# Softmax denominators of a hash-attention kernel: one sum per pair of heads on four quarters of TensorE's columns, spread by transfers

## The chip, the cores and the metric

The kernel runs on one core of a Trainium2 chip. The metric is device time in microseconds (us); the time before is the median of three runs, 891.09 us (890.82 to 892.35). TensorE multiplies matrices (PE in the profile, with PEld for its weight loads), VectorE (DVE), ScalarE (ACT) and GpSimd (POOL) work on elements, and SyncE (SP) issues most transfers. [...]

## What is computed

Hash attention for 4 batches x 8 heads, 768 queries and keys of 64 elements, followed by a feed-forward block with a quick GELU (cut to what matters):

```python
mask = q_bucket[:, :, :, None] == k_bucket[:, :, None, :]      # buckets: 6 sign bits of q @ proj, k @ proj
scores = scale * np.matmul(q, k.transpose(0, 1, 3, 2))
scores = np.where(mask, scores, -1000000000.0)
scores = scores - np.max(scores, axis=-1, keepdims=True)
attn = np.exp(scores)
attn = attn / (np.sum(attn, axis=-1, keepdims=True) + 1e-09)
attn_out = np.matmul(attn, v)
# x: (4 * 768, 512) from attn_out
h = x @ w_in                                   # 512 -> 2048
g = h * (1.0 / (1.0 + np.exp(-1.702 * h)))
out = g @ w_out                                # 2048 -> 512
```

The division by the sum of exponentials is the part that the change touches.

## The kernel before

Two heads make a pair (heads 2hp and 2hp+1 of one batch), so there are 16 pairs, n = 0 to 15. Keys lie on the 128 partitions and queries along the row; the 768 queries of a pair are taken in two halves of 384, c = 0 and c = 1. D is 64, P is 128, T is 6 tiles of 128 keys, GT is 3, HS is 384. One turn of the main loop (a "group") is one half of one pair; for the first pair it is a half of a half.

In group (n, c) TensorE first makes six tiles of scores, each from a product of hash features (bf16, kf and qf) and a product of keys and queries (f32), and ScalarE takes the exponential of each. The sums over keys are made in two parts: GpSimd adds the first three tiles of exponentials, VectorE the last three and GpSimd's result, one group later. What is left, a sum over the 128 partitions, is a product with a matrix of ones on TensorE (`total`), one for each head of the pair.

```python
            def scores(n, c, kts):
                qT, kT, qf, kf = xts[n, "q"], xts[n, "k"], feats[n % 2]["q"], feats[n % 2]["k"]
                cols = slice(c * HS, (c + 1) * HS)
                for kt in kts:
                    ps = sps.tile([P, 2, 512], F32, tag="s", name="ps")
                    keys = slice(kt * P, (kt + 1) * P)
                    for a, m, last in ((kf, qf, False), (kT, qT, True)):
                        for j in range(2):
                            hs = slice(D * j, D * (j + 1))
                            nc.tensor.matmul(ps[:, j, 0:HS], a[hs, keys], m[hs, cols], start=not last, stop=last)
                    nc.scalar.activation(es[c][:, kt, :, 0:HS], ps[:, :, 0:HS], Act.Exp, scale=1.0 / D**0.5)
```
```python
            def add_high(n, c):
                e = [es[c][:, GT + i, :, 0:HS] for i in range(GT)]
                acc = accs[n, c] = st.tile([P, 2, HS], F32, tag="acc", name="acc", bufs=1)
                nc.vector.scalar_tensor_tensor(acc, e[0], T * TINY, e[1], op0=Alu.add, op1=Alu.add)
                for x in (e[2], accs.pop((n, c, 0))):
                    nc.vector.tensor_tensor(acc, acc, x, op=Alu.add)
                # ... (values(): the product of exponentials and v, 12 matmuls into av)
            def x_of(n, c):
                b, hp = pairs[n]
                x = xT[:, hp, b * S : (b + 1) * S]
                x = x.rearrange("d (t p) -> d t p", p=P) if n else x.rearrange("d (p t) -> d t p", p=P)
                return x[:, c * GT : (c + 1) * GT, :]

            def unload(n, c):
                av = avs.pop((n, c))
                vs = st.tile([P, 1], F32, tag="vs", name="vs")
                nc.scalar.copy(vs, av[:, HS : HS + 1])
                nc.scalar.activation(x_of(n, c), av[:, 0:HS].rearrange("p (t s) -> p t s", t=GT), Act.Identity, bias=vs[:, 0:1])

            def total(n, c):
                acc = accs.pop((n, c))
                dn = accs[n, c] = mps.tile([P, HS], F32, tag="m", name="dn")
                for j in range(2):
                    nc.tensor.matmul(dn[D * j : D * (j + 1), :], ones, acc[:, j, :], start=True, stop=True)

            def invert(n, c):


                dn = accs.pop((n, c))
                rt = st.tile([P, HS], F32, tag="rt", name="rt")
                nc.vector.transpose(rt, dn)
                r = st.tile([P, HS // 32, 1], F32, tag="r", name="r")
                nc.vector.reciprocal(r, rt.rearrange("p (s i) -> p s i", i=32)[:, :, 0:1])
                accs[n, c] = rt, r

            def spread(n, c):
                rt, r = accs[n, c]
                nc.vector.transpose(rt.rearrange("p (s i) -> p s i", i=32), r.to_broadcast([P, HS // 32, 32]))

            def norm(n, c):
                rt, r = accs.pop((n, c))
                nc.vector.tensor_tensor(x_of(n, c), x_of(n, c), rt.rearrange("p (t s) -> p t s", t=GT), op=Alu.mult)
```

`total` fills a PSUM tile `dn` whose 64 rows per head are all the same sum, `invert` turns it in blocks of 32x32 so that each sum lies in one element of a row and takes the reciprocal of 12 elements, `spread` turns it back into rows, and `norm` multiplies the output of the attention.

The hash features of the next pair are made in the same groups: `hashed` is a product for four quarters of TensorE's columns (two halves of k, two of q), `featured` makes the features with one VectorE instruction and sends them to their partitions with eight small transfers of 12 partitions each. The first four (kf and qf of half 0 among them) must have landed before the first scores of the next pair.

```python
            def hashed(n):

                h = dots[n] = mps.tile([P, HS], F32, tag="m", name="hash")
                for i, x in enumerate("kq"):
                    for c in range(2):
                        r0 = D * i + 32 * c
                        nc.tensor.matmul(h[r0 : r0 + 32, :], pf[x], xts[n, x][:, c * HS : (c + 1) * HS],
                                         start=True, stop=True)

            def featured(n):
                f = wk.tile([P, HS], BF16, tag="f", name="f", bufs=1)
                nc.vector.tensor_scalar(f, dots.pop(n), above[:, 0:1], weight[:, 0:1], op0=Alu.is_gt, op1=Alu.mult)
                for c in range(2):
                    for i, x in enumerate("kq"):

                        queue = nc.scalar if (n, x) == (1, "q") else nc.sync
                        for j in range(2):
                            r0 = D * i + 32 * c + 2 * NB * j
                            queue.dma_start(out=feats[n % 2][x][D * j : D * j + 2 * NB, c * HS : (c + 1) * HS],
                                            in_=f[r0 : r0 + 2 * NB, :])
```

The weights w_in come as 64-bit floats and are converted in the same groups, one chunk of 128x512 per pair (`convert`, a generator that `step` moves on; each `yield` ends a step):

```python
        raw = cv.tile([P, CW, 2], U32, tag="raw", name="raw")
        (queue or loader[0]).dma_start(out=raw, in_=src)

        def of(x):
            return x if len(dst.shape) == 2 else x.rearrange("p (x r) -> p x r", r=dst.shape[2])

        lo, hi = raw[:, :, 0], raw[:, :, 1]
        bits = cv.tile([P, CW], U32, tag="bits", name="bits")
        part = (cv if psum is None else psum).tile([P, CW], U32, tag="part", name="part")
        size = (cv if psum is None else psum).tile([P, CW], F32, tag="size", name="size")
        yield
        # 1: part = (hi << 3) & mask            VectorE
        # 2: bits = (hi & 0xC0000000) | part    VectorE
        # 3: part = bits & 0xFF800000           VectorE;   size = hi * hi   ScalarE
        # 4: part = lo * 2**-52 * part          VectorE
        # 5: dst = bits + part                  VectorE
        # 6: dst = (size >= ...) * dst          VectorE
```

The loop:

```python

                if hashes:
                    featured(hashes.pop())
                ended = prev and prev[2][-1] == T - 1
                if ended:
                    add_high(*prev[:2])
                    totals.append((g + (g == len(groups) or len(kts) == GT), prev[:2]))
                for x in norms:
                    spread(*x)

                turned = ("", "k", "q", "")[g] if n == 0 else "kq" if c == 0 and n < last else ""
                for x in turned:
                    turn(n + 1, x)
                    measure(n + 1, x)
                if c == 1 or n == 0:
                    while norms:
                        norm(*norms.pop(0))
                inverted = []
                while totals and totals[0][0] == g:
                    inverted.append(totals.pop(0)[1])
                    total(*inverted[-1])
                    invert(*inverted[-1])
                while norms:
                    norm(*norms.pop(0))
                norms += inverted
                if prev:
                    values(*prev)
                if ended:
                    unload(*prev[:2])
                if "q" in turned:
                    hashed(n + 1)
                    if n:
                        hashes.append(n + 1)
                    else:
                        featured(n + 1)
                    for x in "kq":
                        if n + 2 <= last:
                            fetch(n + 2, x)
                    fetch_v(n + 1)
                if kts and kts[-1] == T - 1:
                    step(n, 4 - c)
                    if c == 0 and n > last - len(x_sums):
                        x_sums[n - last - 1]()
                    if c == 1:
                        begin(n + 1)
                if g == len(groups) - 1:
                    guard(0)
                if g == len(groups):
                    guard(1)
```

The transfers of the loop are issued by SyncE, in an order that the program's build has fixed: before the change, for each pair, four of k and four of q (of the pair after the next), two of v, eight of features, one of w_in.

Of the kernel before, what the change touches and what calls it, by code (L numbers as in the profile page):

```python
# [8 lines left out]
F32 = mybir.dt.float32  # L9
# [10 lines left out]
P = 128  # L20
# [18 lines left out]
def kernel(  # L39
# [118 lines left out]
    def convert(cv, dst, src, queue=None, psum=None):  # L158
# [10 lines left out]
        part = (cv if psum is None else psum).tile([P, CW], U32, tag="part", name="part")  # L169
        size = (cv if psum is None else psum).tile([P, CW], F32, tag="size", name="size")  # L170
# [109 lines left out]
    def attention(ff):  # L280
# [4 lines left out]
        with actx:  # L285
# [154 lines left out]
            def add_high(n, c):  # L440
                e = [es[c][:, GT + i, :, 0:HS] for i in range(GT)]
                acc = accs[n, c] = st.tile([P, 2, HS], F32, tag="acc", name="acc", bufs=1)
                nc.vector.scalar_tensor_tensor(acc, e[0], T * TINY, e[1], op0=Alu.add, op1=Alu.add)
                for x in (e[2], accs.pop((n, c, 0))):
                    nc.vector.tensor_tensor(acc, acc, x, op=Alu.add)  # L445
# [10 lines left out]
            def x_of(n, c):  # L456
                b, hp = pairs[n]
                x = xT[:, hp, b * S : (b + 1) * S]
                x = x.rearrange("d (t p) -> d t p", p=P) if n else x.rearrange("d (p t) -> d t p", p=P)
                return x[:, c * GT : (c + 1) * GT, :]  # L460

            def unload(n, c):
                av = avs.pop((n, c))
                vs = st.tile([P, 1], F32, tag="vs", name="vs")
                nc.scalar.copy(vs, av[:, HS : HS + 1])  # L465
                nc.scalar.activation(x_of(n, c), av[:, 0:HS].rearrange("p (t s) -> p t s", t=GT), Act.Identity, bias=vs[:, 0:1])  # L466

            def total(n, c):
                acc = accs.pop((n, c))
                dn = accs[n, c] = mps.tile([P, HS], F32, tag="m", name="dn")  # L470
                for j in range(2):
                    nc.tensor.matmul(dn[D * j : D * (j + 1), :], ones, acc[:, j, :], start=True, stop=True)  # L472

            def invert(n, c):


                dn = accs.pop((n, c))
                rt = st.tile([P, HS], F32, tag="rt", name="rt")
# [3 lines left out]
                accs[n, c] = rt, r  # L482

            def spread(n, c):
                rt, r = accs[n, c]
                nc.vector.transpose(rt.rearrange("p (s i) -> p s i", i=32), r.to_broadcast([P, HS // 32, 32]))

            def norm(n, c):
                rt, r = accs.pop((n, c))
                nc.vector.tensor_tensor(x_of(n, c), x_of(n, c), rt.rearrange("p (t s) -> p t s", t=GT), op=Alu.mult)  # L490
# [34 lines left out]
            for g in range(len(groups) + 2):  # L525
# [13 lines left out]
                if ended:  # L539
                    add_high(*prev[:2])  # L540
                    totals.append((g + (g == len(groups) or len(kts) == GT), prev[:2]))
                for x in norms:
                    spread(*x)
# [5 lines left out]
                if c == 1 or n == 0:  # L549
                    while norms:  # L550
                        norm(*norms.pop(0))
                inverted = []
                while totals and totals[0][0] == g:
                    inverted.append(totals.pop(0)[1])
                    total(*inverted[-1])
                    invert(*inverted[-1])
                while norms:
                    norm(*norms.pop(0))
                norms += inverted
# [14 lines left out]
                if kts and kts[-1] == T - 1:  # L574
                    step(n, 4 - c)
# [12 lines left out]
            for x in norms:  # L588
                spread(*x)
                norm(*x)  # L590
# [408 lines left out]
```

## Time and profile before

| | |
|---|---|
| time | 891.09 us |
| span of the profiled run | 888.7 us |
| TensorE busy | 873.2 us (98%) |
| VectorE busy | 709.3 us (80%) |
| ScalarE busy | 313.9 us (35%) |
| GpSimd busy | 309.7 us (35%) |
| TensorE in the attention (60 to 340 us) | 279.13 of 280 us |
| sum products `dn` (L472) on the last chain | 3% of the span |

The attention takes the first 335 us, the feed-forward block the rest. A row of the groups names the line of the kernel, the engine, the output and inputs, and the mean time of one instruction. An f32 matmul appears as two records, and matmuls on different columns of TensorE lie over each other, so the time of a step is read from the starts of what follows, not from the sum of durations. A transfer's row (SPq) is the time in which SyncE issues it; the data land later.

### The profile page before, as it was taken

Reading aid. Unit: us, or ns where it says so; the run is one execution under the profiler, and the core shown is the slowest. Engines: PE = TensorE matmul, PEld = TensorE weight load, DVE = VectorE, ACT = ScalarE, POOL = GpSimd, SP = SyncE. Lnnn points to the kernel's source line nnn. Section 1 sums busy time; section 2 is a strip of 40 time slices with the busy share of each in tenths; the row PEclk is TensorE's granted clock in tenths of the full one; section 3 lists DMA queues with packets and bytes.
Section 4 is the critical chain, followed back from the end, with each engine's and each line's share of the span. In section 5 each row is a group of like instructions: output and inputs, shape, how many; then the busy total and the mean of one; then the engine's idle time right before and its main releaser. Section 6 shows DMA issues by size and latency. Waiting matters only on the chain.

```text
span 888.7 us, 11969 instructions
## 1 busy us (share of the span) xinstructions
PE 873.2 (98%) x4077; PEld 503.5 (57%) x4077; DVE 709.3 (80%) x1020; ACT 313.9 (35%) x519; POOL 309.7 (35%) x275
## 2 busy tenths in 40 slices
PE   9899999999999999999999999999999999999995
PEld 4444444444444444444444444444888888888884
DVE  4698887888889964777788787888798977897785
ACT  5755666666665642233222223322100000000000
POOL 4243233222333263666434435559932000000000
PEclk9999999999999999999999999999999999999998
DMA  4745544556544103555455545565845665467524
GB/s 103 122 83 84 103 81 81 86 98 96 97 83 82 46 1 107 188 191 189 177 209 194 201 155 202 189 236 194 301 156 190 190 210 216 159 220 237 190 96 97
DMA packets 169477, 132.01 MB, mean 149 GB/s; under 512 B 123936, under 2 KB 138432, under 8 KB 164032
## 3 DMA queue, kind: packets, MB, share of 16 engines
q1 hardware_dynamic: 167712, 129.69, 51.0%
q10 hardware_dynamic: 1696, 1.48, 0.6%
q8 instruction: 34, 0.56, 0.3%
q14 instruction: 35, 0.29, 0.1%
HBM read 79.69 MB, written 50.33 MB: 146 GB/s over the span
## 4 chain that ended last, share of the span: by engine, by line
PE 96%; DVE 2%; DMA 1%; ACTq 0%; issue 0%; SPq 0%; ACT 0%; DVEq 0%
PE product L699 32%; PE product L812 28%; PE ps L429 16%; PE av L453 14%; PE dn L472 3%; PE hash L405 1%; DMA q<-in_q_dram 1%; PE tp L363 0%; ACTq L417 0%; DVE xT L816 0%; PE warm L356 0%; PE hash L370 0%; DVE y L791 0%; DVE acc L445 0%; SPq L325 0%
## 5 line engine op out<-in xcount | busy, mean ns | idle before, releaser
L430 ACT ACTIVATE e<-ps 128x768 f32<-128x768 f32 x192 | 151.5, 813 | 19.3 <-PE ps L429 13.4
L429 PE MATMUL ps<-qT,kT 64*128 64x384 f32 x768 | 155.1, 482 | 0.0
L699 PE MATMUL product<-xT,w_in_sb 128*128 128x512 f32 x288 | 135.4, 592 | 0.0
L453 PE MATMUL av<-e,v 128*64 128x385 f32 x768 | 130.2, 486 | 0.9 <-ACT xT L466 0.9
L437 POOL TENSOR_TENSOR acc<-e 128x768 f32<-128x768 f32 x32 | 49.6, 1551 | 208.1 <-ACT e L430 103.3
L707 ACT ACTIVATE c<-c 128x512 f32<-128x512 f32 x72 | 45.5, 632 | 186.2 <-issue 78.8
L453 PEld LDWEIGHTS av<-e,v 128*64 128x64 f32 x768 | 54.9, 136 | 70.5 <-issue 69.0
L699 PEld LDWEIGHTS product<-xT,w_in_sb 128*128 128x128 f32 x288 | 54.6, 190 | 68.5 <-issue 63.4
L699 PE MATMUL product<-t_x,s_in 128*128 128x512 f32 x192 | 90.2, 592 | 0.0
L429 PEld LDWEIGHTS ps<-qT,kT 64*128 64x128 f32 x768 | 68.2, 188 | 35.5 <-issue 35.5
L216 POOL TENSOR_TENSOR v<-c,u 128x512 f32<-128x512 f32 x24 | 34.3, 1427 | 129.2 <-ACT c L707 129.2
L818 ACT COPY u<-product 128x256 f32<-128x256 f32 x21 | 7.8, 373 | 167.7 <-PE product L812 125.6
L429 PE MATMUL ps<-qf,kf 64*128 64x384 bf16 x384 | 63.0, 324 | 0.7 <-ACT e L430 0.5
L699 PEld LDWEIGHTS product<-t_x,s_in 128*128 128x128 f32 x192 | 36.5, 190 | 45.9 <-issue 43.8
L438 POOL TENSOR_TENSOR acc<-acc,e 128x768 f32<-128x768 f32 x32 | 56.7, 1772 | 2.5
L699 PE MATMUL product<-xT,s_in 128*128 128x512 f32 x96 | 45.1, 592 | 0.0
L699 PE MATMUL product<-t_x,w_in_sb 128*128 128x512 f32 x96 | 45.1, 592 | 0.0
L429 PEld LDWEIGHTS <-kf 64*128 64x128 bf16 x384 | 18.9, 94 | 42.2 <-issue 20.7
L479 DVE STREAM_TRANSPOSE rt<-dn 128x384 f32<-128x384 f32 x32 | 18.6, 580 | 25.7 <-PE dn L472 25.6
L465 ACT COPY vs<-av 128x1 f32<-128x1 f32 x32 | 5.1, 160 | 95.0 <-PE av L453 94.9
L812 PE MATMUL product<-raw_g,xT 128*128 128x256 f32 x152 | 35.1, 379 | 0.0
L490 DVE TENSOR_TENSOR xT<-xT,rt 128x384 f32<-128x384 f32 x32 | 32.6, 1020 | 1.7
(201 smaller groups left out, 1558.3 us busy)
## 6 DMA issues: line engine op xcount, KB each, us to landing
raw_g<-g_dram SPq DMA_DIRECT2D x22, 1024.0 KB
s_in<-g_dram SPq DMA_DIRECT2D x20, 1024.0 KB
g_dram<-c SPq DMA_DIRECT2D x72, 256.0 KB
g_dram<-t SPq DMA_DIRECT2D x48, 256.0 KB
raw<-in_moe_w_out_dram SPq DMA_DIRECT2D x16, 512.0 KB
raw<-in_moe_w_in_dram SPq DMA_DIRECT2D x15, 512.0 KB
v<-in_v_dram SPq DMA_DIRECT2D x32, 192.0 KB
g_dram<-u SPq DMA_DIRECT2D x24, 256.0 KB
```

The costliest lines, as they stand in the source:

```text
L216: return [lambda: eng.tensor_tensor(t1, b12, b11, op=Alu.subtract), lambda: eng.tensor_tensor(b12, b22, b12, op=Alu.subtract), lambda: eng ...
L429: nc.tensor.matmul(ps[:, j, 0:HS], a[hs, keys], m[hs, cols], start=not last, stop=last)
L430: nc.scalar.activation(es[c][:, kt, :, 0:HS], ps[:, :, 0:HS], Act.Exp, scale=1.0 / D**0.5)
L437: nc.gpsimd.tensor_tensor(acc, es[c][:, 0, :, 0:HS], es[c][:, 1, :, 0:HS], op=Alu.add)
L438: nc.gpsimd.tensor_tensor(acc, acc, es[c][:, 2, :, 0:HS], op=Alu.add)
L453: nc.tensor.matmul(av[D * j : D * (j + 1), :], vt[:, t, j, :], es[c][:, t, j, :], start=(t == 0), stop=(t == T - 1))
L472: nc.tensor.matmul(dn[D * j : D * (j + 1), :], ones, acc[:, j, :], start=True, stop=True)
L479: nc.vector.transpose(rt, dn)
L490: nc.vector.tensor_tensor(x_of(n, c), x_of(n, c), rt.rearrange("p (t s) -> p t s", t=GT), op=Alu.mult)
L699: nc.tensor.matmul(ps, wq[LEFT[i]][:, kc, :], xq[RIGHT[i]][:, kc, :], start=(kc == 0), stop=(kc == K2 - 1))
L707: nc.scalar.activation(c, c, Act.Gelu_apprx_sigmoid)
L812: nc.tensor.matmul(ps, wq[LEFT[i]][:, c, :], gq[RIGHT[i]][:, c, :], start=(c == 0), stop=(c == F4 - 1))
```

## The change

Both halves of a pair's queries are summed in one step, at the first group of the next pair. The product of ones uses 32 columns instead of 64, so that head j and half c get the 32 rows from 64j + 32c on, four products on four quarters of TensorE's columns. One pass of `invert` then does both halves and turns the reciprocals back at once; each quarter holds 32 equal rows. Eight transfers of 32 partitions x 384 (48 KB each) copy them to the 64 rows of each head and half in `rs`, and one `norm` per pair multiplies 128x768. It saves sums on TensorE and instructions on VectorE. To make room in SBUF, `convert` keeps `part` in its destination and the square in place of the high word, and its steps are split 2 and 4 over the two groups of a pair, where they were 4 and 3. `acc` gets two buffers, since two are now alive at a time.

```diff
@@ -166,8 +166,11 @@
 
         lo, hi = raw[:, :, 0], raw[:, :, 1]
         bits = cv.tile([P, CW], U32, tag="bits", name="bits")
-        part = (cv if psum is None else psum).tile([P, CW], U32, tag="part", name="part")
-        size = (cv if psum is None else psum).tile([P, CW], F32, tag="size", name="size")
+        if psum is None:
+            part, size = dst.bitcast(U32), hi.bitcast(F32)
+        else:
+            part = psum.tile([P, CW], U32, tag="part", name="part")
+            size = psum.tile([P, CW], F32, tag="size", name="size")
         yield
 
 
@@ -439,7 +442,7 @@
 
             def add_high(n, c):
                 e = [es[c][:, GT + i, :, 0:HS] for i in range(GT)]
-                acc = accs[n, c] = st.tile([P, 2, HS], F32, tag="acc", name="acc", bufs=1)
+                acc = accs[n, c] = st.tile([P, 2, HS], F32, tag="acc", name="acc")
                 nc.vector.scalar_tensor_tensor(acc, e[0], T * TINY, e[1], op0=Alu.add, op1=Alu.add)
                 for x in (e[2], accs.pop((n, c, 0))):
                     nc.vector.tensor_tensor(acc, acc, x, op=Alu.add)
@@ -453,41 +456,44 @@
                         nc.tensor.matmul(av[D * j : D * (j + 1), :], vt[:, t, j, :], es[c][:, t, j, :],
                                          start=(t == 0), stop=(t == T - 1))
 
-            def x_of(n, c):
+            def x_of(n):
                 b, hp = pairs[n]
                 x = xT[:, hp, b * S : (b + 1) * S]
-                x = x.rearrange("d (t p) -> d t p", p=P) if n else x.rearrange("d (p t) -> d t p", p=P)
-                return x[:, c * GT : (c + 1) * GT, :]
+                return x.rearrange("d (t p) -> d t p", p=P) if n else x.rearrange("d (p t) -> d t p", p=P)
 
             def unload(n, c):
                 av = avs.pop((n, c))
                 vs = st.tile([P, 1], F32, tag="vs", name="vs")
                 nc.scalar.copy(vs, av[:, HS : HS + 1])
-                nc.scalar.activation(x_of(n, c), av[:, 0:HS].rearrange("p (t s) -> p t s", t=GT), Act.Identity, bias=vs[:, 0:1])
-
-            def total(n, c):
-                acc = accs.pop((n, c))
-                dn = accs[n, c] = mps.tile([P, HS], F32, tag="m", name="dn")
-                for j in range(2):
-                    nc.tensor.matmul(dn[D * j : D * (j + 1), :], ones, acc[:, j, :], start=True, stop=True)
-
-            def invert(n, c):
-
-
-                dn = accs.pop((n, c))
-                rt = st.tile([P, HS], F32, tag="rt", name="rt")
+                nc.scalar.activation(x_of(n)[:, c * GT : (c + 1) * GT, :], av[:, 0:HS].rearrange("p (t s) -> p t s", t=GT), Act.Identity, bias=vs[:, 0:1])
+
+            def total(n):
+
+                dn = accs[n] = mps.tile([P, HS], F32, tag="m", name="dn")
+                for c in range(2):
+                    acc = accs.pop((n, c))
+                    for j in range(2):
+                        r0 = D * j + 32 * c
+                        nc.tensor.matmul(dn[r0 : r0 + 32, :], ones[:, 0:32], acc[:, j, :], start=True, stop=True)
+
+            def invert(n):
+
+
+                dn = accs.pop(n)
+                rt = st.tile([P, HS], F32, tag="rt", name="rt", bufs=1)
                 nc.vector.transpose(rt, dn)
                 r = st.tile([P, HS // 32, 1], F32, tag="r", name="r")
                 nc.vector.reciprocal(r, rt.rearrange("p (s i) -> p s i", i=32)[:, :, 0:1])
-                accs[n, c] = rt, r
-
-            def spread(n, c):
-                rt, r = accs[n, c]
                 nc.vector.transpose(rt.rearrange("p (s i) -> p s i", i=32), r.to_broadcast([P, HS // 32, 32]))
-
-            def norm(n, c):
-                rt, r = accs.pop((n, c))
-                nc.vector.tensor_tensor(x_of(n, c), x_of(n, c), rt.rearrange("p (t s) -> p t s", t=GT), op=Alu.mult)
+                rs = accs[n] = st.tile([P, 2, HS], F32, tag="rs", name="rs", bufs=1)
+                for c in range(2):
+                    for r0 in range(0, P, 32):
+                        r1 = r0 // D * D + 32 * c
+                        nc.sync.dma_start(out=rs[r0 : r0 + 32, c, :], in_=rt[r1 : r1 + 32, :])
+
+            def norm(n):
+                x, rs = x_of(n), accs.pop(n)
+                nc.vector.tensor_tensor(x, x, rs.rearrange("p c (t s) -> p (c t) s", t=GT), op=Alu.mult)
 
 
             groups = [(n, c, kts) for n in range(len(pairs)) for c in range(2)
@@ -538,25 +544,19 @@
                 ended = prev and prev[2][-1] == T - 1
                 if ended:
                     add_high(*prev[:2])
-                    totals.append((g + (g == len(groups) or len(kts) == GT), prev[:2]))
-                for x in norms:
-                    spread(*x)
+                    if prev[1] == 1:
+                        totals.append((g + (g == len(groups)), prev[0]))
 
                 turned = ("", "k", "q", "")[g] if n == 0 else "kq" if c == 0 and n < last else ""
                 for x in turned:
                     turn(n + 1, x)
                     measure(n + 1, x)
-                if c == 1 or n == 0:
-                    while norms:
-                        norm(*norms.pop(0))
-                inverted = []
-                while totals and totals[0][0] == g:
-                    inverted.append(totals.pop(0)[1])
-                    total(*inverted[-1])
-                    invert(*inverted[-1])
                 while norms:
-                    norm(*norms.pop(0))
-                norms += inverted
+                    norm(norms.pop(0))
+                if totals and totals[0][0] == g:
+                    norms.append(totals.pop(0)[1])
+                    total(norms[-1])
+                    invert(norms[-1])
                 if prev:
                     values(*prev)
                 if ended:
@@ -572,7 +572,7 @@
                             fetch(n + 2, x)
                     fetch_v(n + 1)
                 if kts and kts[-1] == T - 1:
-                    step(n, 4 - c)
+                    step(n, 2 + 2 * c)
                     if c == 0 and n > last - len(x_sums):
                         x_sums[n - last - 1]()
                     if c == 1:
@@ -586,8 +586,7 @@
                     early.close()
                     next(ff)
             for x in norms:
-                spread(*x)
-                norm(*x)
+                norm(x)
 
 
     def shifted_attention():
```

In the order that the build gives SyncE after the change, the eight transfers of `rs` stand after the first transfer of k and before its other three, q, v, the features and w_in.

## The prediction

> **What bounds the kernel now.** I read the page first, then TensorE's waits, then one pair of heads in the timelines of TensorE, SyncE and ScalarE. The page:
>
> ```profile
> PE 873.2 (98%) x4077; PEld 503.5 (57%) x4077; DVE 709.3 (80%) x1020; ACT 313.9 (35%) x519; POOL 309.7 (35%) x275
> ...
> PE 96%; DVE 2%; DMA 1%; ACTq 0%; issue 0%; SPq 0%; ACT 0%; DVEq 0%
> ```
>
> TensorE is the bound; every microsecond taken from it counts, unless something else then ends last. Its longest waits are a few single ones:
>
> ```profile
> PE dn L472 <- DVE acc L445: 1.5, 1, 1.5
> PE warm L356 <- DVE idle L76: 1.2, 1, 1.2
> ```
>
> So in the attention TensorE runs without a pause, and its timeline repeats from pair to pair. One pair, second group (n, 1) from the scores' last tile on, with the hash products of the group before it:
>
> ```profile
> 154.24 0.87 PE L472 MATMUL dn<-acc,ones 128*64 128x384 f32 x4
> 154.93 4.05 PE L453 MATMUL av<-e,v 128*64 128x385 f32 x24
> 158.91 0.52 PE L405 MATMUL hash<-kT,pf_k 128*32 128x384 f32 x2
> ...
> 159.70 0.34 PE L429 MATMUL ps<-qf,kf 64*128 64x384 bf16 x2
> ...
> 164.65 0.87 PE L472 MATMUL dn<-acc,ones 128*64 128x384 f32 x4
> 165.34 4.05 PE L453 MATMUL av<-e,v 128*64 128x385 f32 x24
> 169.33 0.34 PE L429 MATMUL ps<-qf,kf 64*128 64x384 bf16 x2
> ```
>
> From start to start: six score tiles 4.95 us (159.70 to 164.65), sums 0.69 to 0.70, values 3.98, hash products 0.79. A pair starts at 154.24 - 4.95 = 149.29 and the next at 169.33: a period of 20.04 us.
>
> SyncE's timeline of the same pair matters as much:
>
> ```profile
> 156.02 2.04 SPq L325 DMA_DIRECT2D k<-in_k_dram  x4
> 158.17 2.16 SPq L325 DMA_DIRECT2D q<-in_q_dram  x4
> 160.43 1.06 SPq L337 DMA_DIRECT2D v<-in_v_dram  x2
> 161.58 1.53 SPq L417 DMA_DIRECT2D kf<-f  x2
> 163.16 1.49 SPq L417 DMA_DIRECT2D qf<-f  x2
> 164.69 1.47 SPq L417 DMA_DIRECT2D kf<-f  x2
> 166.20 1.81 SPq L417 DMA_DIRECT2D qf<-f  x2
> 168.13 0.57 SPq L162 DMA_DIRECT2D raw<-in_moe_w_in_dram  x1
> ```
>
> It starts 6.73 us after the pair's start, when ScalarE has measured k, and then issues back to back for 12.7 us. The features that the next pair's first score needs (kf and qf of half 0) are issued by 164.65, that is 4.68 us before 169.33. This is the slack into which the change puts eight transfers.
>
> [...] two pairs of f32 products on two tiles take 0.70 us, four on four tiles (hash) 0.79, not 1.4. [...] the last qf was issued by 305.86 + 1.47 = 307.33, and SyncE then waited 1.2 us more for it (first two lines below); I take 1.3 us from the end of issue to a TensorE start. [...] features (12 partitions) take 0.71 to 0.73 us to issue, 128-partition stores 0.32 (last two lines). The new transfers have 32 partitions, so they should be of the 0.32 kind; no run here shows that yet.
>
> ```profile
> 305.86 1.47 SPq L417 DMA_DIRECT2D qf<-f  x2
> ...
> SPq L704 <- DMA qf<-f: 1.2, 1, 1.2
> ...
> L417 SPq DMA_DIRECT2D kf<-f x60: 713/732/1922, 24.0 to 305.1; - x60
> ...
> L704 SPq DMA_DIRECT2D g_dram<-c x72: 319/320/823, 342.5 to 630.5; - x72
> ```
>
> **The change, part by part.**
>
> *TensorE.* Removed per pair: two sums, 2 x 0.70 = 1.40 us. Added: one of four quarters, which has the shape of the hash step, 0.78. Saved 0.62, so a pair needs 20.04 - 0.62 = 19.42 us of TensorE, and 16 pairs would save 9.9 us. That is the intended gain: 881 us.
>
> *VectorE.* Per pair one pass of turn, reciprocal, turn (0.58 + 0.23 + 0.57 = 1.38 us) goes, and two multiplies of 128x384 (mean 1.02) become one of 128x768. VectorE is not the bound in the attention, so this pays nothing by itself.
>
> *SyncE.* Eight transfers of 48 KB come after the first k. Each at 0.32 issue and 0.05 gap (the gap between neighbours above): 8 x 0.37 = 2.95 us. They cannot start before the reciprocals are turned. TensorE's sum starts at 4.95; VectorE's first turn followed it by 0.91 before (154.24 to 155.15) and should by some 0.93 now; turn, reciprocal, turn as a dependent chain took 1.46 us at the end of the attention (347.00 to 348.46). So they start 7.45 us into the pair at the earliest, while the other three k would have been issued from 7.1 on. What follows up to the end of qf of half 0 is as now: 156.43 (second k) to 164.64, 8.2 us, a little less with an emptier queue, 8.15. Then 1.3 to land. Sum: 7.45 + 2.95 + 8.15 + 1.3 = 19.85 us after the pair's start, and TensorE is ready for the features at 19.42. The features come late by 0.4 us.
>
> *The conversion.* Its square on ScalarE moves from the first group to the second, behind the unloading of the values, which waits for TensorE's end of the group. The place in the trace:
>
> ```profile
> 159.03 0.16 ACT L465 COPY vs<-av 128x1 f32<-128x1 f32 x1 [2.07 <-PE av L453]
> 159.22 0.58 ACT L466 ACTIVATE xT<-av,vs 128x384 f32<-128x384 f32 x1
> 159.70 0.66 ACT L187 ACTIVATE size<-raw 128x512 f32<-128x512 f32 x1
> ```
>
> That is, the square ends 1.45 us after TensorE's group (158.91 to 160.36). VectorE's last step of the chunk needs it, and VectorE takes its work in order: last step, three adds of `add_high`, two turns of k and q, then the turn of `dn`. From the last step to that turn is 5.35 us (0.61 + 3 x 1.05 + 2 x 0.87, starts to starts). With a pair's TensorE work ending W = 19.42 after its start and the next pair starting P after it, the last step starts W + 1.5 - P into the next pair, and the eight transfers start at that + 5.35 + 1.54 = 27.8 - P, if this is later than 7.45. With P = 19.42 that would be 8.4.
>
> *The sum.* P is the largest of 19.42, of 7.45 + 12.4, and of (27.8 - P) + 12.4. The last gives P = 20.1, in a steady state or swinging between 19.85 and 20.4. That is 0.06 us more than the 20.04 of now: the late features eat what TensorE saves. It holds for pairs 2 to 13 (12 periods, +0.7 us). In pair 1 the trace of before has a wait of 1.5 us for `acc` that goes, but its k and q come late: VectorE's turn of `dn` began at 36.48, the transfers could start at 38.0 and would end at 41.0, the features land at 41.0 + 8.2 + 1.3 = 50.5, and pair 2 started at 49.07: +1.4. Pairs 14 and 15 fetch no k and q, so they save 0.62 each, -1.2. Sum: 891.1 + 0.7 + 1.4 - 1.2 = 892.0 us.
>
> At the end of the attention the last `norm` now waits on VectorE some 4 us for its eight transfers, beside the first products of the feed-forward block. TensorE has six PSUM tiles of 1.7 us of product each and VectorE idles about 1 us before most of its additions there, so I count nothing for it.
>
> **The rivals.** *A, the intended gain:* the features still come in time, 881 us. It needs the chain behind the sums 1.4 us shorter than I count (8.4 + 12.4 = 20.8 against 19.42, with the square in its place); for it speaks that landing may be shorter and that v is at times delayed by a wait of its own now. *B, the issue of a transfer between two places in SBUF costs what the features cost, 0.75 each:* then 6.0 in place of 2.95, P about 22.9 and 12 periods of +2.9, with pair 1 +4.4: about 929 us. For it speaks that all transfers of this kind in the trace take 0.71 or more; against it that they all have 12 partitions. *C, in between:* the queue is not empty behind the first k (its neighbours take 0.52 where the first takes 0.39), so 0.45 to 0.5 each: P about 20.8, 901 us. *D, VectorE becomes the bound:* against it stands that its work per pair falls to about 15.5 of 20 us; though the multiply of 128x768 may lie beside GpSimd's adds, where the half of it took 1.51 instead of 0.49 us, there is room before the square.
>
> **Range and chances.** My sum at 892, with 0.3 us of doubt per period (landing, gaps) giving 4 us either way; A reaches down to 881, C and B pull upward more. Range 883 to 908. Faster than 873 would need more than the whole saving: 0.02. Slower than 909 needs something near B: 0.12. Within 2%: 0.86.
>
> **What would show it.** Quarter sums from `dn` to `av` of 0.78 us, one per pair: the TensorE term. Issue of `rs` near 0.32: against B. A new line in TensorE's waits, the feature product L432 on the transfers of qf or kf, about a dozen times and 0.4 to 1 us each: the SyncE step; if it is missing and the period is 19.4, A is right and my chain too long. VectorE's last conversion step waiting for ScalarE's square: the conversion step. I am wrong if pairs 2 to 13 have a period outside 19.7 to 20.6, or if TensorE waits in the feed-forward block.

## The result, and the profile after

The changed kernel takes 951.32 us (median of 6 runs, 950.01 to 953.73) against 891.13 us before (6 runs, 890.74 to 892.35): a ratio of 1.0675, 95% interval 1.066 to 1.069. It is slower by 60 us; predicted were 892.0 us, 883 to 908.

First the page of the kernel after, the busy time of each engine and the granted clock in 40 slices:

```profile
PE 895.2 (94%) x4077; PEld 519.6 (55%) x4077; DVE 702.5 (74%) x956; ACT 314.0 (33%) x519; POOL 319.0 (34%) x275
...
PEclk9989999989899899999999999999999999999998
```

TensorE runs as many products as before (4077), and its busy time has grown by 22 us (873.2 before) although each pair has fewer sums to do. The clock row shows where that may come from: it dips again and again in the first two fifths of the span, the attention, and then not until the last slice. The first of TensorE's waits (time in all, how many, the longest):

```profile
PE ps L432 <- DMA qf<-f: 38.9, 24, 5.2
```

Before there was no wait for features. The two findings, 38.9 us of waits and 22 us more of busy time (what the fewer sums save is already off it), make up the 60 us. TensorE's only wait for VectorE in the feed-forward block is one of 0.6 us.

One pair of heads in TensorE's timeline, from the sums of one pair to the first product of the next:

```profile
177.79 0.85 PE L477 MATMUL dn<-acc,ones 128*32 128x384 f32 x8
178.58 4.10 PE L456 MATMUL av<-e,v 128*64 128x385 f32 x24
182.61 0.52 PE L408 MATMUL hash<-kT,pf_k 128*32 128x384 f32 x2
...
183.40 0.34 PE L432 MATMUL ps<-qf,kf 64*128 64x384 bf16 x2
...
188.34 4.10 PE L456 MATMUL av<-e,v 128*64 128x385 f32 x24
195.91 0.47 PE L432 MATMUL ps<-qf,kf 64*128 64x384 bf16 x1 [3.46 <-DMA qf<-f]
```

Quarter sums 0.79 (177.79 to 178.58), values 4.03, hash products 0.79, six score tiles 4.94: every piece has the length that was predicted for it. Then TensorE stands for 3.46 us until the features of the next pair land. The same queue in SyncE's timeline, in the pair that starts at 148.68 us:

```profile
158.25 5.01 SPq L492 DMA_DIRECT2D rs<-rt  x8
163.30 1.73 SPq L328 DMA_DIRECT2D k<-in_k_dram  x3
...
168.56 1.60 SPq L420 DMA_DIRECT2D kf<-f  x2
170.21 1.47 SPq L420 DMA_DIRECT2D qf<-f  x2
```

The eight new transfers hold the queue for 5.05 us, not 2.95, and they wait for the sums. So what stands behind them moves by more than they take: the second k starts 14.6 us into the pair (163.30), where before it started 7.1 us into it (156.43). The features of half 0 were issued by 164.65 before (in a pair that started at 149.29, 15.4 us into it); here they are issued by 171.68, 23.0 us into it. The next pair starts at 172.30.

**The chain, term by term.** In the twelve periods from 52.56 us (pair 2) to 347.20 us (pair 14) a pair's start depends on the same chain each time: sums, reciprocals, eight transfers, the rest of the queue, landing. Each term is read from the two timelines; the queue is split into what it takes when nothing disturbs it (158.25 to 163.30 and 163.30 to 171.68 above) and what it took beyond that.

| term of the chain, us | predicted | measured, mean of 12 | difference x 12 |
|---|---|---|---|
| pair's start to its sums | 4.95 | 7.36 | +28.9 |
| sums to the first transfer | 2.50 | 2.41 | -1.1 |
| eight transfers | 2.95 | 5.05 | +25.2 |
| queue up to qf of half 0 | 8.15 | 8.38 | +2.8 |
| single transfers and gaps of the queue that took longer | 0 | 0.77 | +9.3 |
| end of issue to TensorE's start | 1.30 | 0.59 | -8.6 |
| sum | 19.85 | 24.56 | +56.5 |

Twelve periods took 294.6 us, that is 24.55 each. Two terms failed by much: the transfers' issue, and the time from a pair's start to its sums, six score tiles whose length I had taken as fixed. The second is a matter of the clock. Windows of the same kernel on the score tiles of two pairs, the first two from the pair at 148.68, the last two from the pair at 172.30 (length, busy time of PE, PEld, DVE, ACT and POOL, granted clock, DMA share, GB/s):

```profile
148.70:150.40 1.70, 1.48 (x10) 0.97 (x12) 1.67 (x3) 0.12 (x1) 0.00 (x0) 1.00 0.06 15
150.40:153.40 3.00, 3.00 (x14) 1.70 (x12) 2.90 (x4) 1.77 (x3) 1.04 (x1) 0.50 0.27 46
172.30:174.00 1.70, 1.46 (x10) 0.97 (x12) 1.67 (x3) 0.08 (x1) 0.00 (x0) 1.00 0.12 26
174.00:177.80 3.80, 3.80 (x29) 2.21 (x26) 3.14 (x4) 3.74 (x5) 2.08 (x2) 1.00 0.46 134
```

Both pairs began with a wait of 1.8 us and another of 0.2 us (1.82 and 0.22 in the first, 1.81 and 0.24 in the second). In the first the clock falls to 0.50 some 1.7 us after the start, at 150.40, and stays there until 153.82. Its second line counts 14 records of products in 3.0 us, the second pair's last line 29 in 3.8 us at full clock. The sums began 7.16 us after the start of the first pair and 5.49 us after that of the second.

Why one wait lowers the clock and the other does not can be read from the clock's own record. In this run it changed only at marks that lie whole multiples of 3.413 us apart: all 25 changes do (the falls at 126.51, 150.40 and 194.77, for example, lie 23.89 and 44.37 us apart, 7 and 13 times 3.413). What separates the two pairs is TensorE's standing between two neighbouring marks:

```profile
146.99:150.40 3.41, 1.51 (x10) 1.02 (x12) 2.37 (x4) 1.32 (x4) 0.00 (x0) 1.00 0.14 27
170.88:174.29 3.41, 1.75 (x12) 1.16 (x14) 2.37 (x3) 1.33 (x3) 0.00 (x0) 1.00 0.08 17
```

Of the first stretch TensorE stands 1.90 us, of the second only 1.66 us, because the mark at 170.88 cuts the wait before the pair in two. In the attention of this run twelve stretches at full clock have 1.90 us or more of standing, and each is followed by one or two stretches at 0.50; after none with 1.66 us or less does the clock fall.

### The profile page after: what moved, and what is told of

It reads as the page before. It is cut to its first block, busy times and chain, and to the rows that moved or that the text cites. A ratio compares the mean times of both kernels' runs of the same rounds, so it can differ in the third digit from the quotient of the medians.

```text
span 949.4 us, 12081 instructions
## 1 busy us (share of the span) xinstructions
PE 895.2 (94%) x4077; PEld 519.6 (55%) x4077; DVE 702.5 (74%) x956; ACT 314.0 (33%) x519; POOL 319.0 (34%) x275
## 4 chain that ended last, share of the span: by engine, by line
PE 73%; SPq 11%; DVE 7%; DMA 5%; issue 2%; POOL 1%; ACT 0%; ACTq 0%; DVEq 0%; POOLq 0%
PE product L698 29%; PE product L811 26%; PE ps L432 12%; SPq L492 5%; PE av L456 3%; SPq L420 3%; DMA qf<-f 3%; SPq L328 2%; DMA rs<-rt 2%; DVE w_in_sb L186 1%; PE dn L477 1%; DVE xT L496 1%; DVE w_in_sb L193 1%; DVE w_in_sb L178 1%; DVE rt L484 1%
## 5 line engine op out<-in xcount | busy, mean ns | idle before, releaser
L432 PE MATMUL ps<-qT,kT 64*128 64x384 f32 x768 | 180.7, 541 | 0.0
L440 POOL TENSOR_TENSOR acc<-e 128x768 f32<-128x768 f32 x32 | 55.2, 1725 | 258.5 <-DVE acc L448 150.4
L432 PE MATMUL ps<-qf,kf 64*128 64x384 bf16 x384 | 78.4, 356 | 40.1 <-DMA qf<-f 38.9
L432 PEld LDWEIGHTS ps<-qT,kT 64*128 64x128 f32 x768 | 82.0, 211 | 44.2 <-issue 44.1
L456 PEld LDWEIGHTS av<-e,v 128*64 128x64 f32 x768 | 52.1, 136 | 77.6 <-issue 75.5
L432 PEld LDWEIGHTS <-kf 64*128 64x128 bf16 x384 | 26.0, 102 | 80.0 <-DMA kf<-f 44.7
L441 POOL TENSOR_TENSOR acc<-acc,e 128x768 f32<-128x768 f32 x32 | 60.7, 1896 | 3.3 <-ACT e L433 1.3
L484 DVE STREAM_TRANSPOSE rt<-dn 128x384 f32<-128x384 f32 x16 | 9.3, 580 | 55.4 <-PE dn L477 55.3
L446 DVE SCALAR_TENSOR_TENSOR acc<-e 128x768 f32<-128x768 f32 x32 | 31.8, 994 | 6.4 <-ACT e L433 6.4
```

The lines of the kernel that those rows point to most:

```text
L440: nc.gpsimd.tensor_tensor(acc, es[c][:, 0, :, 0:HS], es[c][:, 1, :, 0:HS], op=Alu.add)
L441: nc.gpsimd.tensor_tensor(acc, acc, es[c][:, 2, :, 0:HS], op=Alu.add)
L456: nc.tensor.matmul(av[D * j : D * (j + 1), :], vt[:, t, j, :], es[c][:, t, j, :], start=(t == 0), stop=(t == T - 1))
```

## The experiments

Two causes had to be told apart and weighed: the queue (transfers delay the features, TensorE waits) and the clock (the wait lowers TensorE's speed afterwards). Beside them stood the moved conversion steps, which the prediction had put on the chain, and the question why one transfer takes 0.63 us with its gap. Each edit below is against the changed kernel; each time stands beside runs of the kernel before on the same chip (medians 890.9 to 891.6 us).

### e1_no_transfers: the sums in quarters, no transfers

It leaves out the spreading: both halves of queries are multiplied with `rt` as it is, so half of the rows get another row's reciprocal.

```diff
-                rs = accs[n] = st.tile([P, 2, HS], F32, tag="rs", name="rs", bufs=1)
-                ... eight nc.sync.dma_start(out=rs[...], in_=rt[...])
+                accs[n] = rt
-                nc.vector.tensor_tensor(x, x, rs.rearrange("p c (t s) -> p (c t) s", t=GT), op=Alu.mult)
+                both = rt.rearrange("p (o t s) -> p o t s", o=1, t=GT).to_broadcast([P, 2, GT, P])
+                nc.vector.tensor_tensor(x, x, both, op=Alu.mult)
```

> The changed kernel with the eight transfers per pair left out: the multiply takes the reciprocals of rt as they lie, so part of the rows get a wrong divisor; all the rest of the change stays. Theory 1 (queue): the transfers stand ahead of the features on SyncE's queue, the features come late, TensorE waits 2 to 5 us per pair, and for some microseconds after such a wait its matmuls take up to twice as long; without the transfers the period falls from 23.6 to 25.5 us to 19.42 and the time to 881 (878 to 885). Theory 2 (conversion): the square on ScalarE behind the unloading, and VectorE's order, hold TensorE up; then the time stays above 930. Theory 3 (traffic): the bytes of the transfers delay the features on the DMA engines; then also 881, and it is told apart by the next kernel.

Measured: 885.16 us, ratio 0.9932 (0.9915 to 0.9948). TensorE has no wait for features left, and a pair takes 19.72 us. So the transfers cost all of the 60 us and the 6 us that the rest of the change brings. It brings less than the 9.9 us intended: here the sums take longer than their 0.78 us before the values start:

```profile
171.49 1.04 PE L477 MATMUL dn<-acc,ones 128*32 128x384 f32 x8
172.46 0.87 PE L456 MATMUL av<-e,v 128*64 128x385 f32 x4
```

### e4_old_steps and e5_old_steps_no_transfers: the conversion steps split as before

```diff
-                    step(n, 2 + 2 * c)
+                    step(n, 4 - c)
```

e4 is the changed kernel with this line; e5 has it beside the edit of e1, and leaves out what e1 leaves out.

> The changed kernel with the conversion's steps split 4 and 3 over the two groups as before the change, so that the square on ScalarE comes in the first group. Theory 1: VectorE turns the sums as soon as TensorE has them (it waits for them 3 us in the profile), so the square is not on the chain and the time stays 951 (946 to 956). Theory 2 (conversion): it falls under 930. The prediction's own step, in which the square sets the start of the transfers, would give a gain of up to 0.9 us per pair, 940 to 946.

> The changed kernel without the eight transfers (as in the first experiment, so with some wrong divisors) and with the conversion's steps split 4 and 3 as before the change. In the first experiment the quarter sums took 0.97 us from start to the values, not 0.78. Theory C (the second pair of quarter products waits for VectorE's adds, which stand behind the last conversion step, which waits for the square on ScalarE): with the square in the first group the sums take 0.78, 15 times 0.19 us less, and the time is 882 (881 to 883.5) against 885.2. Rival (quarter products simply cost 0.97 when TensorE comes to them without a pause): the time stays 885 (884 to 886).

Measured: e4 948.3 us, ratio 1.0637 (1.0619 to 1.0654), 3.0 us less than the changed kernel; e5 883.17 us, ratio 0.9904 (0.9889 to 0.9919), 2.0 us less than e1. The moved square costs 2 to 3 us, with or without the transfers, so not by delaying them. In e5 the sums take 0.78 us again (171.13 to 171.91 in its timeline), so the 0.19 us of e1 belong to the order of the steps: VectorE's adds for the second half's sums stand behind the last conversion step there. With them right a pair takes 19.54 us: e5 shows what the quarters are worth when nothing pays for the spreading, 8.2 us.

### e3_filled_wait: TensorE kept busy while it waits

Twelve products on idle data, whose result nobody reads, at the end of every pair from 1 to 14. The kernel computes all it did, with the transfers as in the changed kernel.

```diff
+                    if c == 1 and 1 <= n < last:
+                        fill = mps.tile([P, HS], F32, tag="m", name="fill")
+                        for _ in range(FILL):          # FILL = 12
+                            nc.tensor.matmul(fill, idle[:, 0:P], idle[:, 0:HS], start=True, stop=True)
```

> The changed kernel with 12 idle matmuls (bf16, 384 columns, about 2 us in all) on TensorE at the end of each pair, where it would wait for the features; their result is not used. In the changed kernel the waits add up to about 37 us and the slow score tiles after them to about 32 us. Theory 1a (the slow tiles are a lower clock that follows on idle time of TensorE): the tiles come back to 0.81 us, the sums and so the transfers come about 2.2 us earlier in each pair, and the time falls by 22 to 32 us, to 919 to 929. Rival 1b (the slow tiles wait for features of the second half or for transfers): they stay slow, and the time is 948 to 958.

Measured: 929.92 us, ratio 1.0432 (1.0414 to 1.0449), so 21.4 us less than the changed kernel, with more work on TensorE. The mean clock is 0.996 where the changed kernel has 0.968, and from 60 to 340 us it is 1.00 against 0.92. TensorE's waits for qf have fallen from 38.9 to 11.8 us. The longest is one of 3.12 us that ends at 52.75; after it one score tile takes 1.60 us (55.41 to 57.01), where the tiles of the pair at 169.20 take 0.81. No other wait for qf is over 1.15 us. The timeline in one of the waits:

```profile
166.77 2.12 PE L584 MATMUL fill<-idle 128*128 128x384 bf16 x12
169.20 0.32 PE L433 MATMUL ps<-qf,kf 64*128 64x384 bf16 x1 [0.30 <-DMA qf<-f]
169.82 0.32 PE L433 MATMUL ps<-qf,kf 64*128 64x384 bf16 x1 [0.31 <-DMA qf<-f]
```

The chain of the table, read in the same way over twelve periods: start to sums 5.70 (7.36), sums to transfer 2.41 (2.41), the eight transfers and the rest of the queue with its long transfers 14.15 (14.20), landing 0.64 (0.59), in all 22.90 us (24.56). Only the first term has moved, by 1.66 us; 12 x 1.66 = 19.9 us of the 21.4. This separates the two causes: some 20 us are lost because the clock drops after the wait, and the other 39 us (929.9 against 891) remain with the clock held. Of the first term 0.75 us remain above 4.95, in the pair above 0.46 of it as the wait for the second transfer of qf, between the two first products (169.20 and 169.82 instead of side by side).

### e7_half_the_transfers: four transfers instead of eight

Only the reciprocals of the first half are spread, and both halves use them, so half of the output has wrong divisors.

```diff
-                for c in range(2):
+                for c in range(1):
                     for r0 in range(0, P, 32):
                         ... nc.sync.dma_start(out=rs[...], in_=rt[...])
+                both = rs[:, 0].rearrange("p (o t s) -> p o t s", o=1, t=GT).to_broadcast([P, 2, GT, P])
```

> The changed kernel with four of the eight transfers at the same place, those of half 0; the multiply uses them for both halves, so half of the outputs get a wrong divisor. Theory 1 with 1a (chain on SyncE's queue, and a lower clock only after waits of some 2 us): the chain is 2.5 us shorter, the features come within 0.5 us of TensorE's need, no slow tiles follow, and the time is 888 (884 to 894). Rival (each transfer costs its share): half of the loss remains, 915 to 921.

Measured: 895.91 us, ratio 1.0054 (1.0039 to 1.007), just above the expected range. TensorE waits 5.0 us for qf, 7 times (once 3.3 us), and 1.7 us for kf, and the clock is 0.994. The first four transfers cost 10.7 us over e1, the next four 55.4: the cost is not proportional to the number. Up to the slack of the queue they cost little, beyond it each 0.63 us counts in full in every period, and the clock adds its share.

### e6_issue_costs: what a transfer costs the queue, by kind

The kernel of e1 (with what it leaves out) and, after the attention, a row of transfers from `rt` to `rs` and to a tile `d_room` in DRAM, whose results nobody reads.

```diff
+                    nc.sync.dma_start(out=rs[r0 : r0 + 32, c, :], in_=rt[r1 : r1 + 32, :])           # L532
+                    nc.sync.dma_start(out=rs[:, c, :], in_=rt)                                       # L534
+                    nc.sync.dma_start(out=d_room[c, r0 : r0 + 32, :], in_=rt[r0 : r0 + 32, :])       # L537
+                    nc.sync.dma_start(out=d_room[c], in_=rt)                                         # L539
+                    nc.sync.dma_start(out=rs[r0 : r0 + 16, c, 0:192], in_=rt[r0 : r0 + 16, 0:192])   # L542
+                    nc.sync.dma_start(out=rs[r0 : r0 + 12, c, 0:192], in_=rt[r0 : r0 + 12, 0:192])   # L545
```

> The changed kernel without the eight transfers per pair, with some transfers added in a quiet stretch of SyncE's queue at the end of the attention, to read their issue times: rt to rs (SBUF to SBUF) in blocks of 32 rows of 1536 bytes and in whole tiles of 128 rows, rt to DRAM in the same two shapes, rt to rs in 16 and in 12 rows of 768 bytes. If the place decides (SBUF to SBUF), the first two take about 0.58 and the DRAM ones about 0.32; if the number of rows decides, the 128-row ones take 0.32 and the 32-row ones 0.58 wherever they go. [...] The time itself should be that of the first experiment, 885.

Measured: 886.59 us in its one run, near the 885 expected. The time of one issue in ns (least, median, most), transfers into SBUF and then into DRAM:

```profile
L532 SPq DMA_DIRECT2D rs<-rt x8: 584/588/590, 312.9 to 317.4; - x8
L542 SPq DMA_DIRECT2D rs<-rt x8: 507/588/591, 323.9 to 328.8; - x8
L545 SPq DMA_DIRECT2D rs<-rt x8: 713/714/781, 329.5 to 334.9; - x8
L534 SPq DMA_DIRECT2D rs<-rt x2: 518/518/518, 318.1 to 319.9; - x2
```

```profile
L537 SPq DMA_DIRECT2D d_room<-rt x8: 414/422/592, 318.7 to 323.0; - x8
L539 SPq DMA_DIRECT2D d_room<-rt x2: 349/406/463, 323.5 to 325.9; - x2
```

32 rows within SBUF cost 588 ns, as in the changed kernel, and the same rows into DRAM 422: the place they go to makes 0.17 us. 128 rows instead of 32 save 0.07 (518). 12 rows cost 0.13 more than 16 of the same length (714 and 588): rows do count, as the prediction had it, but this is the smaller part. All this is one run at one time of the queue: the kinds stand side by side in it, and the absolute figures hold for it alone.

### e2_transfers_later and e8_later_and_old_steps: the same transfers behind the features

The eight transfers go out in the second group, once the features are issued, and the multiply follows at the first group of the pair after; the result is complete. e8 has the old step split besides, and the multiply behind the next reciprocals instead of ahead of them.

```diff
+            def send(n):               # the eight transfers, as before
                 ...
                     featured(hashes.pop())
+                if c == 1 and sends:
+                    send(sends.pop())
...
-                while norms:
-                    norm(norms.pop(0))
+                if c == 0:
+                    while norms and norms[0] not in sends:
+                        norm(norms.pop(0))
```

> The changed kernel with the same eight transfers issued one group later, behind the eight feature transfers of the next pair, and the multiply another group later; the result is that of the reference. Theory 1 (queue): features are issued as before the change, 4.7 us ahead of their use, the period is 19.42 us and the time 883 (880 to 888), under the kernel before. Theory 2: above 930. Theory 3 (traffic): as many bytes move in each pair, so at least half of the loss stays: above 910.

> The kernel with the transfers behind the next pair's features, with the conversion's steps split 4 and 3, and with the multiply behind the turns of the sums instead of ahead of them; the result is that of the reference. The version with transfers behind the features lost 3.7 us against the one without transfers, where VectorE waited for the transfers ahead of the turns and the square ahead of the adds. Theory: both waits leave the chain, period 19.45 us, time 884 (882 to 886.5), under the kernel before by 0.8%. If SyncE's queue itself, some 17.6 us of issue in 19.5, is what holds it, it stays at 888 to 890.

Measured: e2 888.84 us, ratio 0.9979 (0.9972 to 0.9987); e8 893.64 us, ratio 1.0025 (1.0015 to 1.0036), against an expectation of 884. In e2 the same 5.00 us of issue stand behind the last qf:

```profile
186.35 1.47 SPq L420 DMA_DIRECT2D qf<-f  x2
187.87 5.00 SPq L496 DMA_DIRECT2D rs<-rt  x8
```

Same transfers, same bytes, another place in the queue: 62 us less. So it is their place ahead of the features that costs, not their traffic. The rest of the gain (e1 has 885.16) is not there: SyncE's queue is full for 18.2 of 19.7 us in most pairs, and VectorE waits 23.2 us for `rs`, 9.5 of them once at the end; how much each of these costs was not separated. In e8 VectorE waits in another place, 22.3 us in 11 times, since the next turn of `dn` into the one buffer of `rt` has to wait until the transfers have read it:

```profile
217.54 0.58 DVE L484 STREAM_TRANSPOSE rt<-dn 128x384 f32<-128x384 f32 x1 [2.53 <-DMA rs<-rt]
```

My expectation for e8 had missed that wait. A second buffer of `rt` was not tried.

### e9_other_queue: the same transfers from GpSimd's queue

The transfers go out at the same point as in the changed kernel, but from GpSimd; the multiply stands at the next pair's first group, and the steps are split as before. The result is complete.

```diff
-                        nc.sync.dma_start(out=rs[r0 : r0 + 32, c, :], in_=rt[r1 : r1 + 32, :])
+                        nc.gpsimd.dma_start(out=rs[r0 : r0 + 32, c, :], in_=rt[r1 : r1 + 32, :])
...
-                while norms:
-                    norm(norms.pop(0))
+                if c == 0:
+                    while norms:
+                        norm(norms.pop(0))
...
-                    step(n, 2 + 2 * c)
+                    step(n, 4 - c)
```

> The changed kernel with the eight transfers at the same moment and with the same bytes, but issued from GpSimd's queue instead of SyncE's, with the multiply one group later and the conversion's steps split 4 and 3; the result is that of the reference. Theory 1 (only the place on SyncE's queue matters): the features are issued as before the change, TensorE never waits for them, the period is 19.45 to 19.6 us and the time 883 to 886. Theory 3 (traffic at that moment) or a GpSimd whose issue of transfers makes its adds late: above 890.

Measured: 883.47 us (882.55 to 884.56), ratio 0.9905 (0.9888 to 0.9922) to the kernel before. It beats both kernels and equals e5, which has no transfers at all (883.17). The transfers of a pair in GpSimd's timeline:

```profile
193.67 3.93 POOL L492 DMA_DIRECT2D rs<-rt  x8 [1.00 <-DVE rt L487]
```

GpSimd had waited for the reciprocals and issues the eight in 3.93 us, 496 ns each, in time that it had free; SyncE's queue holds none of them, and TensorE waits for no features. A pair takes 19.53 us. Beside e4 (948.3 us, the same step split) only the queue and the place of the multiply differ; the place of the multiply is not what gains, since e5 has it where the change put it and takes as long as e9. This is the confirmation of the queue as the root from the other side: with the delay gone, the waits and the clock's dips are gone as well (mean clock 0.996). What is gone is time of issue on SyncE: in the changed kernel 8 x 0.63 us of it stood ahead of a transfer that TensorE waits for.

## Why the prediction was wrong

- **The bound and the slack: right.** TensorE bounds the kernel, the features on SyncE's queue are the thing to watch, and the slack of 4.68 us was read rightly. That a wait L432 on qf would appear was named as the sign; it came, at 1.8 to 3.5 us a pair instead of 0.4 to 1.
- **The TensorE term: right.** The quarter sums take 0.78 to 0.79 us. Without transfers a pair takes 19.54 us (e5), against the 19.42 predicted.
- **"Each at 0.32 issue and 0.05 gap": the step that failed first.** It is 0.588 and 0.04. I took 0.32 from stores of 128 partitions into DRAM and estimated that 12 against 128 partitions is the whole of the difference to the features' 0.72; nothing in the profile showed that, and it had no transfer of 32 rows within SBUF. In e6 the destination makes 0.17 us, 32 rows instead of 128 make 0.07, and 12 instead of 16 make 0.13. Over twelve periods the mistake is 25.2 us. Rival B, with 0.75, had the right kind and the nearest time (929 us), the time in part by luck: its 6.0 us for the eight are too much, and it lacks the clock. I gave its neighbourhood a chance of 0.12, because I took the 12 rows as excluding other reasons.
- **Six score tiles as a fixed 4.95 us: the step that failed unseen.** The chain starts with them, and the wait at its end slows them: the clock drops after it. e3 takes 20 us of this away. It added 1.66 us to a period that had grown by 2.86 us without it (22.90 in e3, 20.04 before). No rival contained it. In the trace the clock falls to 0.50, at marks 3.413 us apart that do not follow the kernel's waits; 1.90 us of standing between two marks were enough, 1.66 us were not. So 2.0 us of waiting, in two pieces, counted in the pair at 148.68 and not in the one at 172.30.
- **Single long transfers in the queue: not foreseen.** One transfer of q took up to 2.30 us after the change and at most 0.61 in the same stretch before; the twelve periods lose 9.3 us to such, gaps between transfers included. e3 has them as well. What makes them long was not settled.
- **Landing 1.3 us: too long, by 0.71.** The 1.3 us was counted from the end of the second transfer of qf, but the first product needs only the first one, and follows the end of its issue by 1.37 us on average. The second product then waits for the other one, which belongs to what the first score tile has lost.
- **The conversion: the mechanism failed.** The prediction had its square push the transfers back to 8.4 us after the start. In all twelve periods the transfers follow the sums by 2.40 to 2.41 us, so nothing on VectorE held them. The sign named for it came all the same: VectorE waits 11.8 us for the square, 13 times; but it then has time over, since it waits 55.3 us for the sums. The square costs 2 to 3 us in another place, as e4 and e5 show, in e5 at the sums.
- **The feed-forward block: nearly right.** VectorE waits 9.7 us for the last `rs` there, not some 4, and TensorE 0.6 us for VectorE; I had counted nothing.

The sum: twelve periods at 24.55 instead of 20.1 us are 53.4 us, pair 2 starts 2.1 us later than predicted (52.56 against 50.5), pair 14 takes 22.24 instead of 19.42 us, 2.8 more, and the feed-forward 0.6. Together 58.9 of the 59.3 us between 892.0 and 951.3. Two sums of the prediction do not add up as written, and neither decides anything: 4.95, 0.93 and 1.46 make 7.34, not 7.45, and the parts given for 5.35 make 5.50 (three adds from start to start take 3.00, not 3 x 1.05).

## What to carry to other kernels

Before transfers are added to a queue, add their issue times and compare the sum with the slack of the first urgent transfer behind them; take the issue time from one of the same kind (both ends, rows: in e6 32 rows into DRAM took 422 ns, 12 rows within SBUF 714), and if the profile has none, let the range cover the dearest kind in it. A wait on TensorE can cost more than its own length: of two pairs here that had waited 2.0 us, one had its sums 7.16 us after its start, with the clock at 0.50 for 3.4 us, and the other after 5.49 us at full clock; they differ in where the wait lay between the clock's marks. Transfers that nobody waits for soon belong behind the urgent ones, or on the queue of an engine that has time, which here turned a loss of 6.7% into a gain of 1%.

## What the runs showed of the hardware that was not expected

- In the changed kernel the granted clock changed only at marks that lie multiples of 3.413 us apart (all 25 changes). In the attention it fell to 0.50, for 3.4 or 6.8 us, after each of the twelve stretches between marks in which TensorE had stood for 1.90 us or more, and not after 1.66 us; so of two pairs that had waited 2.0 us, one was slowed and the other not.
- On SyncE the issue of 32 rows took 588 ns into SBUF and 422 into DRAM (medians of e6); from GpSimd's queue the same transfer into SBUF took 496 (e9).
- Holding the clock with idle products (2.12 us of them per pair, e3) was worth 21.4 us, though nothing else in the chain moved.
